# Attention norms with tokens on the partitions from block 4 on, in a fused attention and two-layer kernel

## The chip, the cores and the metric

The kernel runs on one core of one Trainium2 chip. The metric is the device time of one execution in microseconds; lower is better. Before the change three runs took 282.09, 282.47 and 282.67 us (median 282.47). The profiled execution took 282.48 us, and its span, from the first to the last instruction, is 280.7 us.

## What is computed

An attention without a softmax, a norm over each head, and a two-layer net with a leaky ReLU that has a slope of its own for each hidden unit:

```python
kv = np.einsum('bhsd,bhse->bhde', k, v)          # 8 batches, 8 heads, 576 tokens, 64 wide
out = np.einsum('bhsd,bhde->bhse', q, kv)
rms = np.sqrt(np.mean(out * out, axis=-1, keepdims=True) + 1e-06)
x = out / rms * g_norm                           # then to (4608 tokens, 512)
h = x @ w_in                                     # 512 -> 2048
g = np.maximum(h, 0.0) + alpha * np.minimum(h, 0.0)
return g @ w_out                                 # 2048 -> 512
```

Inputs and output are fp32; the matmuls run on fp16 copies with fp32 sums.

## The kernel before

**Blocks and units.** The 4608 tokens are worked on in nine blocks w of 512 (L39). A batch has 576 tokens, so a block spans a batch boundary in most cases. The main loop (L781) goes over the blocks, and inside a block over 16 units u (L784). A unit holds one first-layer group, `m1_group` (four 512-column matmuls on TensorE, L391; a ReLU of the negative on ScalarE, L398; the combination `gt` on VectorE, L402), seven 256-column matmuls of the second layer of the block before (`prod_mm`, L523; the product is done by a scheme with seven instead of eight sub-products, which needs sums of `gt` quarters, `s_sum`, L489, 16 a block on VectorE), and a piece of the attention for the block after (`attention(w + 1, u)`, L764). So the norms of block 4 are computed in the loop of block 3.

**Attention of a block, channels on partitions.** Heads go in pairs j = 0 to 3 (two heads of 64 fill 128 partitions). `step_kv` (L323) makes the 128x128 product kv of a pair from five matmuls, and VectorE copies it under a mask (L335). `step_ot` (L340) multiplies kv by the transposed queries: 512 columns for each pair, in two matmuls where the block spans two batches; the result has channels on partitions and tokens along the row. ScalarE squares it (L355). `ssq_mm` (L362) sums the squares over the 64 channels of a head with a 512-column matmul against a 0/1 mask (L365), and ScalarE takes the reciprocal root of all 128x512 values (L367). `norm` (L372) multiplies on VectorE by the gain `g2col` and by the root, and writes `xt`, the moving operand of the first layer, one tile for each pair. The units of these steps are written out by hand: kv at 1, 4, 7, 10, the product at 3, 6, 9, 12, sum and norm at 5, 8, 11, 14 (L753).

**Queries.** Batches 0 to 2 are transposed on TensorE (`step_t`, L287). From batch 3 on (`B_NAT`) `dma_t` (L312) sends five DMA transposes from SyncE's queue, each of 128 (the last of 64) tokens by 512 channels; the loop of block 1 issues those of batch 3 in unit 3 (L790), later loops those of batch w + 2 in unit 11 (L815).

**Order and buffers.** Each engine runs its instructions in the order of the program text, SyncE's and GpSimd's queues too. From block 2 on the first-layer results go to two PSUM banks in turn (L793), so a unit's first matmul waits until `gt` two units before has been computed. The attention products have two PSUM buffers ("o"). GpSimd issues the loads (L180); the load of the query remainder of batch w + 2 waits until the transposes of the batch before have read the shared buffer (L158). SyncE's queue also carries the output stores (L427).

Of the kernel before, what the change touches and what calls it, by code (L numbers as in the profile page):

```python
# [9 lines left out]
FP32 = mybir.dt.float32  # L10
FP16 = mybir.dt.float16
AF = mybir.ActivationFunctionType
ALU = mybir.AluOpType
# [4 lines left out]
def kernel(  # L18
# [11 lines left out]
    nc = tc.nc  # L30

    B, H, S, D = q.shape
# [3 lines left out]
    P = 128  # L36
    NPAIR = H // 2
    W = 512
    NW = N_TOK // W  # L39
    TPW = W // P  # L40
    TPP = S // P
    MAIN = TPP * P
    REM = S - MAIN
    NT = TPP + 1
# [3 lines left out]
    NC = D_MODEL // P  # L48
    assert NC == NPAIR and 0 < REM < P and P0 <= P and H % 4 == 0
    B_NAT = 3  # L50
    inv_d = 1.0 / D

    const_p = ctx.enter_context(tc.tile_pool(name="constp", bufs=1))
    w_p = ctx.enter_context(tc.tile_pool(name="weights", bufs=1))
    xt_p = ctx.enter_context(tc.tile_pool(name="xt", bufs=2))
# [63 lines left out]
    NBUF = 3  # L119
    HH = H // 2  # L120
    bufs = []
    for i in range(NBUF):
        t = {}
        for nm in ("k", "v", "q"):
            n = 1 if nm == "v" else T0 if i == 0 else NT
            t[nm] = qkv_p.tile([P, n, H, D], FP16, name=f"{nm}sb{i}")
            if i > 0 or nm == "v":
                nc.vector.memset(t[nm][REM:P, n - 1, :, :], 0.0)
        bufs.append(t)
# [26 lines left out]
            )  # L156

    def buf_of(b, nm):  # L158
        return bufs[1 if nm == "q" and b >= B_NAT else b % NBUF][nm]

    def load_rem(b, nm):
        nc.gpsimd.dma_start(  # L162
# [2 lines left out]
        )  # L165

    def regroup(b, nm, h0, h1, eng=None):
        dst = bufs[b % NBUF][nm][:, 0:TPP, h0:h1, :].rearrange("p t h d -> p h t d")
        src = stages[b, nm][:, h0:h1, :, :]
        if eng is nc.scalar:  # L170
            nc.scalar.copy(out=dst, in_=src)
        else:
            (eng or nc.vector).tensor_copy(out=dst, in_=src)

    def load_batch(b, names=("k", "v", "q")):
        for nm in names:
            load_rem(b, nm)
            load_main(b, nm)
# [30 lines left out]
    def load_w_in(i):  # L209
# [4 lines left out]
        )  # L214
        w_in_sb.append(t)

    def load_w_out(i):
        t = w_p.tile([P, GW, D_MODEL], FP16, name=f"w_out_sb{i}")
        nc.gpsimd.dma_start(
            out=t[:],  # L220
            in_=moe_w_out[i * GW * P : (i + 1) * GW * P, :].rearrange("(g p) m -> p g m", p=P),
        )
        w_out_sb.append(t)

    def w_in_blk(c, g):
        i = max(n for n, f0 in enumerate(IN_CUTS[:-1]) if f0 <= g * P)
        f0 = g * P - IN_CUTS[i]
        return w_in_sb[i][:, c, f0 : f0 + P]
# [20 lines left out]
    load_batch(1, ("v",))  # L249
    load_w_out(2)  # L250
    load_w_out(3)
    load_batch(2, ("q", "k", "v"))


    warm_ps = ps_q.tile([P, W], FP32, name="warm_ps", tag="q")
# [18 lines left out]
    def pair_cols(b, nm, j):  # L274
        def f(t):
            n = rows(b)
            if nm == "v" and b == 0:
                h = 2 * j % HH
                return stages[b, nm, 2 * j // HH][0:n, h : h + 2, t, :]
            if nm == "v" and t < TPP:  # L280
                return stages[b, nm][:, 2 * j : 2 * j + 2, t, :]
            if nm == "v":
                return bufs[b % NBUF][nm][0:n, 0, 2 * j : 2 * j + 2, :]
            return bufs[b % NBUF][nm][0:n, t, 2 * j : 2 * j + 2, :]
        return f

    def step_t(b, j, pool=(ps_s, "s")):  # L287
        qs = pair_cols(b, "q", j)
        qt_ps = pool[0].tile([P, n_runs(b) * rows(b)], FP16, name="qt_ps", tag=pool[1])
        c = 0  # L290
        for t in range(n_runs(b)):
            n = rows(b)
            nc.tensor.matmul(  # L293
                out=qt_ps[:, c : c + n],
                lhsT=qs(t),
                rhs=ident16[0:n, 0:n],
                is_transpose=True,
                start=(t == 0),
                stop=(t == n_runs(b) - 1),
            )  # L300
            c += n
        if j == 0:
            qt_all[b] = attn_p.tile([P, NPAIR, S], FP16, name="qt_all")
        qts[b, j] = qt_all[b][:, j, :]
        if b == 0 and j < 2:
            nc.vector.tensor_copy(out=qts[b, j], in_=qt_ps[:, 0:S])
        else:
            nc.scalar.copy(out=qts[b, j], in_=qt_ps[:, 0:S])

    qt_all = {}  # L310

    def dma_t(b):  # L312
        qt = attn_p.tile([P, NPAIR, S], FP16, name="qt_all")
        for t in range(NT):
            c0, c1 = t * P, min((t + 1) * P, S)
            src = stages[b, "q"][:, t] if t < TPP else buf_of(b, "q")[0:REM, TPP]
            nc.sync.dma_start_transpose(
                out=qt[:, :, c0:c1], in_=src.rearrange("p h d -> p (h d)"),
            )
        for j in range(NPAIR):  # L320
            qts[b, j] = qt[:, j, :]

    def step_kv(b, j, pool=(ps_s, "s")):  # L323
        ks, vs = pair_cols(b, "k", j), pair_cols(b, "v", j)
# [46 lines left out]

    def norm(w, j):  # L372
        ot_ps, rstd = ots.pop((w, j))
        xts[w, j] = xt_p.tile([P, W], FP16, name="xt", tag=f"xt{j}")
        nc.vector.scalar_tensor_tensor(  # L375
            out=xts[w, j][:], in0=ot_ps[:], scalar=g2col[:], in1=rstd[:],
            op0=ALU.mult, op1=ALU.mult,
        )

    gts = {}  # L380
# [8 lines left out]
    def m1_mm(h_ps, w, g, cs):  # L389
        for c in cs:  # L390
            nc.tensor.matmul(  # L391
                out=h_ps[:], lhsT=w_in_blk(c, g), rhs=xts[w, c][:],
                start=(c == 0), stop=(c == NC - 1),
            )

# [11 lines left out]
    def m1_group(w, g, pool=None):  # L407
        h_ps = pool[0].tile([P, W], FP32, name="h_ps", tag=pool[1]) if pool else h_bank()
        m1_mm(h_ps, w, g, range(NC))
        m1_evac(h_ps, w, g)  # L410
# [248 lines left out]
    ssq_mm(0, 3, h_at(2))  # L659
    norm(0, 2)  # L660
    norm(0, 3)
    first = [ps_h.tile([P, W], FP32, name="h_ps", tag=f"h{g}") for g in range(3)]
    for c in range(3):
        for g in range(2):
# [6 lines left out]
    for g in range(3, NF):  # L671
        m1_group(0, g, {3: S_POOL, 4: O_POOL, 5: O_POOL, 6: Q_POOL}.get(g))
        if g == 14:
            regroup(1, "k", 0, H)
            nc.vector.memset(bufs[0]["k"][REM:P, TPP, :, :], 0.0)


    ys = {}
# [65 lines left out]
        13: ((0, 1, 2), (0, 2, 2)),  # L744
    }

    def unit_sums(w, u):
        for back, n, k in S_AT.get(u, ()):
            if 1 <= w + back < NW:
                s_sum(w + back, n, k)  # L750

# [9 lines left out]
            ATT_1.setdefault(at, []).append((what, j))  # L761
    ATT = {"t": step_t, "kv": step_kv, "ot": step_ot, "ssq": step_ssq}

    def attention(w, u):  # L764
        if w < NW:
            for what, j in (ATT_1 if w == 2 else ATT_AT).get(u, ()):
                if what == "t" and w >= B_NAT:
                    continue
                if w < B or what in ("ot", "ssq"):
                    if w == 2 and what in ("kv", "ssq"):  # L770
                        pool = Q_POOL if j % 2 == 0 else S_POOL
                        (step_kv if what == "kv" else step_ssq)(w, j, pool)
                    else:
                        ATT[what](w, j)

    REG_AT = {8 + 2 * j: (("k", j),) for j in range(NPAIR)}

    Y3_AT = [(8, 8), (8, 8), (8, 8), (8, 9), (9, 9), (9, 10), (10, 10), (10, 10), (10, 11), (11, 11), (11, 12), (12, 12), (12, 13), (13, 14), (14, 16), (16, 16)]
    REG_2 = {2 * j: (("k", j),) for j in range(NPAIR)}
# [1 line left out]
    for w in range(1, NW):  # L781
        if w + 2 < B:
            load_gated(w + 2)
        for u in range(NF):  # L784
            m1_group(w, G_ORDER[u])
            if w > 1:
                unit_sums(w, u)
            if w == 1 and u == 2:
                regroup(2, "k", 0, H)
            if w == 1 and u == 3:  # L790
                dma_t(3)
            if w == 2 and u == 0:
                h_tags[0] = ("h1", "h2")  # L793
                h_turn[0] = 1
            if w > 2 and u == 0:
                y_read(w - 2, "c12")
            if w == 1:
                for i in range(*Y3_AT[u]):
                    y_mm(ys[3], 0, 3, i)
                    if i == NF - 1:  # L800
                        y_out(ys[3], 0, 3)
            else:
                for i in range(u * PER, (u + 1) * PER):
                    prod_mm(w - 1, *Y_LIST[i])
                for what in Y_READS.get(u, ()):
                    y_read(w - 1, what)
            attention(w + 1, u)
            if w == 1:
                for k in {5: (0,), 7: (1,)}.get(u, ()):
                    s_sum(1, 1, k)  # L810
                    s_sum(1, 2, k)
            if w + 2 < B:
                for nm, j in REG_AT.get(u, ()) if w > 1 else ():
                    regroup_pair(w + 2, nm, j)
                if u == 11 and w > 1:  # L815
                    dma_t(w + 2)
            if w == 2:
                for nm, j in REG_2.get(u, ()):
                    regroup_pair(3, nm, j)
                if u < 2:  # L820
                    s_sum(1, u + 1, 2)
# [48 lines left out]
```

## Time and profile before

| what | value |
|---|---|
| span of the profiled execution | 280.7 us |
| TensorE busy, granted clock | 274.0 us (98%), 1.0 throughout |
| VectorE, ScalarE, GpSimd busy | 219.9, 157.0, 61.9 us |
| loop of block 2 to 6, each | 28.89 us |
| loop of block 7, of block 8 | 27.77, 25.06 us |
| mask-sum matmuls L365 | 36 in all, 4 in a loop with attention |
| ScalarE roots L367, squares L355 | 690 and 598 ns each, 36 of each |
| VectorE norms L375 | 745 ns each, 36 |
| DMA transposes | 25, 2.3 us from issue to landing in the median |

In the profile a matmul's busy time overlaps with the next one's, so TensorE's cost is read from start to start. VectorE's instructions overlap a little too: the mean of one is longer than the distance between two that follow at once. A loop's length is the distance between the first first-layer matmuls of two blocks.

### The profile page before, as it was taken

The numbers are of one execution on the slowest core, as the hardware profiler recorded it, in microseconds if no ns is written. First come the engines' busy times: TensorE is split into PE (matmuls) and PEld (weight loads), VectorE is DVE, ScalarE is ACT, GpSimd is POOL, SyncE is SP. The second block draws the span as 40 slices with busy tenths as digits, with TensorE's granted clock in tenths as the row PEclk, the third lists the DMA queues.
The fourth block names the chain that finished last, engine by engine and source line by source line (L and its number), as shares of the span: only waits on it lengthen the run. The fifth ranks groups of instructions, "written<-read, shape, count | busy, mean of one in ns | idle before, by whom it ended". The sixth has DMA issues, their size and how long they took to land.

```text
span 280.7 us, 4978 instructions
## 1 busy us (share of the span) xinstructions
PE 274.0 (98%) x1888; PEld 173.8 (62%) x1888; DVE 219.9 (78%) x418; ACT 157.0 (56%) x268; POOL 61.9 (22%) x85
## 2 busy tenths in 40 slices
PE   7899999999999999999999999999999999999995
PEld 3444444555666676666666666666666666666784
DVE  6668729898788877887889787978887888787872
ACT  3567437788676545764576456745564566443310
POOL 8843332740720046007300450000000000000000
PEclk9999999999999999999999999999999999999999
DMA  8999999999793469947953697330112011201223
GB/s 163 199 207 196 197 201 193 191 140 169 91 171 69 104 72 165 152 112 120 165 91 97 121 152 122 93 106 1 40 37 75 2 37 37 77 0 37 77 76 114
DMA packets 77628, 31.37 MB, mean 112 GB/s; under 512 B 45780, under 2 KB 77284, under 8 KB 77604
## 3 DMA queue, kind: packets, MB, share of 16 engines
q0 software_dynamic: 55600, 18.85, 58.8%
q1 hardware_dynamic: 21108, 11.25, 15.0%
q10 hardware_dynamic: 896, 0.95, 1.0%
q8 instruction: 15, 0.25, 0.4%
q14 instruction: 9, 0.07, 0.1%
HBM read 36.71 MB, written 9.44 MB: 164 GB/s over the span
## 4 chain that ended last, share of the span: by engine, by line
PE 92%; DMA 5%; DVE 1%; ACT 0%; issue 0%; DVEq 0%
PE h_ps L391 42%; PE yY L546 15%; PE yZ L546 10%; PE yX L546 10%; DMA vst<-in_v_dram 5%; PE kv_ps L327 3%; PE ot_ps L349 3%; PE ssq_ps L365 3%; PE y L416 2%; PE warm_ps L259 2%; PE qt_ps L293 1%; DVE xt L375 1%; ACT rstd L367 0%; DVE kv_sb L335 0%; DVE ksb L193 0%
## 5 line engine op out<-in xcount | busy, mean ns | idle before, releaser
L391 PE MATMUL h_ps<-xt,w_in_sb 128*128 128x512 f16 x576 | 145.2, 379 | 0.2
L402 DVE SCALAR_TENSOR_TENSOR gt<-m_sb,beta_sb,h_ps 128x512 f16<-128x512 f32 x144 | 106.9, 746 | 39.9 <-ACT m_sb L398 38.1
L398 ACT ACTIVATE m_sb<-h_ps 128x512 f32<-128x512 f32 x144 | 86.0, 598 | 74.8 <-PE h_ps L391 60.2
L391 PEld LDWEIGHTS <-w_in_sb 128*128 128x128 f16 x576 | 54.8, 98 | 46.4 <-issue 1.0
L546 PEld LDWEIGHTS <-s 128*128 128x128 f16 x512 | 50.1, 98 | 19.3
L546 PEld LDWEIGHTS <-gt 128*128 128x128 f16 x384 | 37.6, 98 | 14.8
L546 PE MATMUL yY<-wsum,s 128*128 128x256 f16 x256 | 36.3, 273 | 0.0
L546 PE MATMUL yX<-w_out_sb,gt 128*128 128x256 f16 x256 | 35.1, 273 | 0.0
L355 ACT ACTIVATE sq_sb<-ot_ps 128x512 f16<-128x512 f32 x36 | 21.2, 598 | 16.7 <-PE ot_ps L349 16.6
L367 ACT ACTIVATE rstd<-ssq_ps,eps_t 128x512 f32<-128x512 f32 x36 | 24.7, 690 | 9.7 <-PE ssq_ps L365 9.2
L375 DVE SCALAR_TENSOR_TENSOR xt<-ot_ps,g2col,rstd 128x512 f16<-128x512 f32 x36 | 26.6, 745 | 3.2 <-ACT rstd L367 3.2
L162 POOL DMA_DIRECT2D qsb<-in_q_dram x7 | 4.9, 699 | 78.3 <-DMA qt_all<-qsb 76.3
L153 POOL DMA_DIRECT2D qst<-in_q_dram x20 | 17.7, 922 | 1.9 <-DMA vst<-in_v_dram 1.9
L546 PE MATMUL yZ<-wsum,s 128*128 128x256 f16 x128 | 17.6, 273 | 0.0
L546 PE MATMUL yZ<-w_out_sb,s 128*128 128x256 f16 x128 | 17.6, 273 | 0.0
L546 PE MATMUL yY<-wsum,gt 128*128 128x256 f16 x128 | 17.6, 273 | 0.0
L416 PE MATMUL y<-w_out_sb,gt 128*128 128x512 f16 x64 | 16.8, 379 | 0.5 <-DMA w_out_sb<-in_moe_w_out_dram 0.5
L349 PE MATMUL ot_ps<-qt_all,kv_sb 128*128 128x512 f16 (+7 forms) x64 | 13.6, 286 | 0.4 <-DVE kv_sb L335 0.3
L498 DVE TENSOR_TENSOR s<-s,gt 128x512 f16<-128x512 f16 x32 | 13.5, 421 | 0.5
L327 PEld LDWEIGHTS <-ksb 128*128 128x128 f16 (+1 forms) x164 | 11.5, 98 | 3.7 <-DVE ksb L193 1.1
L365 PE MATMUL ssq_ps<-sq_sb,mask 128*128 128x512 f16 x36 | 13.6, 379 | 0.1
L496 DVE TENSOR_TENSOR s<-gt 128x512 f16<-128x512 f16 x32 | 13.3, 419 | 0.1
(66 smaller groups left out, 206.6 us busy)
## 6 DMA issues: line engine op xcount, KB each, us to landing
out_dram<-y_sb SPq DMA_DIRECT2D x19, 256.0 KB, 2.2
kst<-in_k_dram POOLq DMA_DIRECT2D x7, 512.0 KB, 7.8
vst<-in_v_dram POOLq DMA_DIRECT2D x7, 512.0 KB, 9.9
qst<-in_q_dram POOLq DMA_DIRECT2D x20, 128.0 KB, 7.2
w_out_sb<-in_moe_w_out_dram POOLq DMA_DIRECT2D x4, 512.0 KB, 16.1
out_dram<-y_sb SPq DMA_DIRECT2D x25, 64.0 KB, 4.2
w_in_sb<-in_moe_w_in_dram POOLq DMA_DIRECT2D x3, 512.0 KB, 11.6
out_dram<-y_sb SPq DMA_DIRECT2D x9, 128.0 KB, 2.1
```

Of the source, the lines that this page charges most:

```text
L153: nc.gpsimd.dma_start(out=st[:, t, :, :], in_=srcs["q"][b, :, t * P : (t + 1) * P, :].rearrange("h p d -> p h d"),)
L327: nc.tensor.matmul(out=kv_ps[:], lhsT=ks(t), rhs=vs(t), start=(t == 0), stop=(t == n_runs(b) - 1),)
L349: nc.tensor.matmul(out=ot_ps[:, n0 - w * W : n1 - w * W], lhsT=kvs[b, j][:], rhs=qts[b, j][:, n0 - b * S : n1 - b * S], start=True, stop=True,
L355: nc.scalar.activation(out=sq[:], in_=ot_ps[:], func=AF.Square)
L365: nc.tensor.matmul(out=ssq_ps[:], lhsT=mask16[:], rhs=sq[:], start=True, stop=True)
L367: nc.scalar.activation(out=rstd[:], in_=ssq_ps[:], func=AF.Abs_reciprocal_sqrt, bias=eps_t[:], scale=inv_d,)
L375: nc.vector.scalar_tensor_tensor(out=xts[w, j][:], in0=ot_ps[:], scalar=g2col[:], in1=rstd[:], op0=ALU.mult, op1=ALU.mult,)
L391: nc.tensor.matmul(out=h_ps[:], lhsT=w_in_blk(c, g), rhs=xts[w, c][:], start=(c == 0), stop=(c == NC - 1),)
L398: nc.scalar.activation(out=m_sb[:], in_=h_ps[:], func=AF.Relu, scale=-1.0)
L402: nc.vector.scalar_tensor_tensor(out=gts[w, i][:, r, :], in0=m_sb[:], scalar=beta_sb[:, g : g + 1], in1=h_ps[:], op0=ALU.mult, op1=ALU.add,)
L416: nc.tensor.matmul(out=y[:], lhsT=gt_cols(w, g, a * P, (a + 1) * P), rhs=w_out_blk(g), start=(g == 0), stop=(g == NF - 1),)
L546: nc.tensor.matmul(out=bank, lhsT=lhs, rhs=rhs, start=fresh, stop=(c == NK - 1), skip_group_check=True,)
```

## The change

From block 4 on (`W_ROW = 4`) the attention product, its norm and the transposition of the result are done another way; block 4 to 8 are 20 tiles of 128 tokens.

- `rows_mm`: for each tile of 128 tokens four 128-column matmuls (one for each pair), with the transposed queries as the stationary and kv as the moving operand, fill one "o" bank with tokens on partitions and all 512 channels along the row. A tile that spans two batches takes two matmuls for each pair, the halves of the query tile being padded with zeros; there are two such tiles. ScalarE squares the bank.
- `rows_ssq`: VectorE sums the squares of each head (`tensor_reduce`, 128x512 to 128x8), two units later.
- `rows_rs`, `rows_norm`: three units after the product ScalarE takes the root of 128x8 values, VectorE multiplies the bank by the roots spread over each head, and SyncE's queue sends a DMA transpose of the 128x512 result into `xt`, now one tile of all four pairs. The mask matmul and the wide root are gone for these blocks.
- The gain moves into `w_in`: in the loop of block 2, VectorE scales the 128x4x128 weights of each group in place, right after that group's evacuation, so `norm` of block 3 leaves the gain out.
- In the loops of blocks 3 to 7 kv moves to units 0, 0, 1, 2 (the second one in an "o" buffer), products to 3, 5, 7, 9, sums of squares to 5, 7, 9, 11, roots and norms to 6, 8, 10, 12; six of the `gt` sums move to later units and two to earlier ones (from unit 6 to 4). The query transposes of batch w + 2 are spread over units 8, 9, 10 and 12, after the result transposes of the same unit; those of batches 3 and 4 go to unit 12.
- The transposed queries lie in two fixed buffers with zeroed padding; batch 2 uses batch 0's query buffer, so its loads stand later in the program; k regroups on ScalarE move from units 8, 10, 12, 14 to 9, 11, 13, 15.

```diff
@@ -213,6 +214,14 @@
+    def scale_w_in(g):
+        ...
+        blk = w_in_sb[i][:, :, f0 : f0 + P]
+        nc.vector.tensor_scalar(
+            out=blk, in0=blk, scalar1=g2col[:], scalar2=None, op0=ALU.mult,
+        )
@@ -249,7 +258,6 @@
-    load_batch(2, ("q", "k", "v"))
@@ -371,10 +378,72 @@
     def norm(w, j):
         ot_ps, rstd = ots.pop((w, j))
-        xts[w, j] = xt_p.tile([P, W], FP16, name="xt", tag=f"xt{j}")
+        if w >= W_ROW - 1:
+            nc.vector.tensor_mul(out=xt_cols(w, j), in0=ot_ps[:], in1=rstd[:])
+            return
         nc.vector.scalar_tensor_tensor(
-            out=xts[w, j][:], in0=ot_ps[:], scalar=g2col[:], in1=rstd[:],
+            out=xt_cols(w, j), in0=ot_ps[:], scalar=g2col[:], in1=rstd[:],
             op0=ALU.mult, op1=ALU.mult,
+        )
+
+    def rows_mm(w, i):
+        n0 = w * W + i * P
+        b, r = divmod(n0, S)
+        o_ps = ps_o.tile([P, W], FP32, name="or_ps", tag="o")
+        for j in range(NPAIR):
+            cols = o_ps[:, j * P : (j + 1) * P]
+            if r + P <= S:
+                c = PAD + r
+                nc.tensor.matmul(
+                    out=cols, lhsT=qt_sb[b % 2][:, j, c : c + P], rhs=kvs[b, j][:],
+                    start=True, stop=True,
+                )
+            else:
+                ...
+        sq = attn_p.tile([P, W], FP16, name="sq_sb")
+        nc.scalar.activation(out=sq[:], in_=o_ps[:], func=AF.Square)
+        ...
+    def rows_ssq(w, i):
+        ...
+        nc.vector.tensor_reduce(
+            out=ssq[:], in_=sq[:].rearrange("p (h d) -> p h d", h=H),
+            axis=mybir.AxisListType.X, op=ALU.add,
+        )
+        ...
+    def rows_rs(w, i):
+        ...
+        nc.scalar.activation(
+            out=rstd[:], in_=ssq[:], func=AF.Abs_reciprocal_sqrt, bias=eps_t[:], scale=inv_d,
+        )
+        ...
+    def rows_norm(w, i):
+        ...
+        nc.vector.tensor_tensor(
+            out=xr[:], in0=o_ps[:].rearrange("p (h d) -> p h d", h=H),
+            in1=rstd[:].unsqueeze(2).to_broadcast([P, H, D]), op=ALU.mult,
+        )
+        xt_cols(w, 0)
+        nc.sync.dma_start_transpose(
+            out=xts[w][:, :, i * P : (i + 1) * P], in_=xr[:].rearrange("p h d -> p (h d)"),
         )
@@ -672,7 +742,11 @@
         if g == 14:
             regroup(1, "k", 0, H)
-            nc.vector.memset(bufs[0]["k"][REM:P, TPP, :, :], 0.0)
+            for nm in ("k", "q"):
+                nc.vector.memset(bufs[0][nm][REM:P, TPP, :, :], 0.0)
+            for t in qt_sb:
+                nc.vector.memset(t[:, :, 0:PAD], 0.0)
+                nc.vector.memset(t[:, :, PAD + S : PAD + S + PAD], 0.0)
@@ -744,8 +818,16 @@
+    S_ROW = dict(S_AT)
+    for at, what in (
+        (4, ((-1, 3, 3), (0, 1, 0), (0, 2, 0))), (6, ()), (7, ((-1, 4, 0),)), (8, ((-1, 4, 1),)),
+        (9, ()), (10, ((-1, 4, 2),)), (11, ()), (12, ((-1, 4, 3),)),
+        (13, ((0, 1, 1), (0, 2, 1))), (15, ((0, 1, 2), (0, 2, 2))),
+    ):
+        S_ROW[at] = what
@@ -761,8 +843,27 @@
+    for what, ats in (
+        ("kv", (0, 0, 1, 2)), ("mm", (3, 5, 7, 9)), ("ssq", (5, 7, 9, 11)),
+        ("rs", (6, 8, 10, 12)), ("norm", (6, 8, 10, 12)),
+    ):
+        for j, at in enumerate(ats):
+            ATT_ROW.setdefault(at, []).append((what, j))
+    QT_AT = {8: (0,), 9: (1,), 10: (2,), 12: (3, 4)}
...
@@ -783,12 +884,12 @@
             m1_group(w, G_ORDER[u])
+            if w == W_ROW - 2:
+                scale_w_in(G_ORDER[u])
...
-            if w == 1 and u == 3:
-                dma_t(3)
@@ -805,6 +906,8 @@
             attention(w + 1, u)
+            if w == 1 and u == 12:
+                dma_t(3)
@@ -812,7 +915,7 @@
-                if u == 11 and w > 1:
+                if u == 12 and 1 < w < W_ROW - 1:
                     dma_t(w + 2)
```

## The prediction

> **What bounds the kernel now.** I read the page's busy line and chain first, then the windows of single loops, then the timeline of one loop.
>
> ```profile
> PE 274.0 (98%) x1888; PEld 173.8 (62%) x1888; DVE 219.9 (78%) x418; ACT 157.0 (56%) x268; POOL 61.9 (22%) x85
> ...
> PE 92%; DMA 5%; DVE 1%; ACT 0%; issue 0%; DVEq 0%
> ```
>
> The chain of waits that ended last is 92% TensorE (PE). The windows (busy time of each engine, one row for each loop of blocks 2 to 7) show the same without a gap:
>
> ```profile
> 66.83:95.72 28.89, 28.89 (x209) 19.42 (x208) 24.06 (x47) 19.65 (x35) 7.32 (x9) 1.00 0.90 115
> 95.72:124.61 28.89, 28.89 (x210) 19.50 (x208) 23.65 (x46) 17.38 (x31) 7.33 (x9) 1.00 0.99 126
> 124.61:153.51 28.90, 28.90 (x211) 19.46 (x208) 23.66 (x46) 17.39 (x31) 7.32 (x9) 1.00 0.88 115
> ...
> 211.29:239.06 27.77, 27.77 (x186) 18.00 (x184) 22.89 (x42) 15.65 (x27) 0.00 (x0) 1.00 0.11 38
> ```
>
> TensorE is busy for the whole of each loop at full clock, so a loop is as long as its matmuls. VectorE (third engine) is busy 23.7 of 28.9 us: 5.2 us are free, so it is the next bound. What each matmul costs is read from starts in the timeline of TensorE:
>
> ```profile
> 137.00 0.38 PE L349 MATMUL ot_ps<-qt_all,kv_sb 128*128 128x320 f16 x2
> 137.22 1.03 PE L391 MATMUL h_ps<-xt,w_in_sb 128*128 128x512 f16 x4
> 138.08 0.93 PE L546 MATMUL yY<-wsum,s 128*128 128x256 f16 x7
> 138.85 0.39 PE L327 MATMUL kv_ps<-vst,ksb 128*128 128x128 f16 x4
> 139.07 0.22 PE L327 MATMUL kv_ps<-vsb,ksb 128*128 128x128 f16 x1
> 139.12 1.03 PE L391 MATMUL h_ps<-xt,w_in_sb 128*128 128x512 f16 x4
> ```
>
> Start to start: 512 columns 0.216 us (0.86/4), 256 columns 0.109 (0.77/7), five 128-column matmuls 0.27, so 0.056 each; the product of one pair 0.22. A bare unit is 4 x 0.216 + 7 x 0.109 = 1.63 us. VectorE's timeline:
>
> ```profile
> 140.82 0.75 DVE L402 SCALAR_TENSOR_TENSOR gt<-m_sb,beta_sb,h_ps 128x512 f16<-128x512 f32 x1 [0.62 <-ACT m_sb L398]
> 141.48 0.42 DVE L502 TENSOR_TENSOR s<-gt,s 128x512 f16<-128x512 f16 x1
> ...
> 143.56 0.42 DVE L502 TENSOR_TENSOR s<-gt,s 128x512 f16<-128x512 f16 x1
> 143.90 0.68 DVE L568 TENSOR_TENSOR u<-yY,p 128x512 f32<-128x512 f32 x1
> 144.51 0.75 DVE L402 SCALAR_TENSOR_TENSOR gt<-m_sb,beta_sb,h_ps 128x512 f16<-128x512 f32 x1
> ```
>
> Start to start: `gt` 0.66, a sum 0.34, an output addition (L568) 0.61. Unit by unit, `gt` can start 1.05 us after the unit's last first-layer matmul (140.82 against 139.12 + 3 x 0.216).
>
> **What the skill says.** "VectorE: DVE Perf Modes", section The perf-mode tier table: `tensor_reduce` has the 1x mode only, `tensor_scalar` on fp16 in SBUF the 4x mode; its section on the TRN2 errata prices an SBUF instruction at (58 + elements/mode)/0.96 ns. The trace agrees where it can: a 512-element sum at 2x gives 0.340 us (measured 0.34), the 2048-element copy L173 at 4x 0.594 (measured 0.60 start to start). No row shows a reduce. "TensorE: Matmul & The Clock Gate", Back-to-back issue gap, has N/2.4 + 2.5 ns for an isolated matmul, 56 ns at 128 columns, but about 81 ns in a stream with weight loads. The kv matmuls here, each with its own weights, take 56, and the measurement decides. "DMA: Bandwidth & Descriptors", Anatomy of one DMA, gives about 2.0 us fixed for a DMA; the 25 transposes here land after 2.3 us in the median, 5.0 at most.
>
> **The change part by part**, for the five loops of blocks 3 to 7; u+0 is the start of unit u's last first-layer matmul.
>
> *TensorE.* Removed: 20 mask matmuls x 0.216 = 4.32 us, and 20 pair products x 0.219 = 4.38. Added: 18 tiles x 4 and 2 boundary tiles x 8 = 88 matmuls x 0.056 = 4.93. Sum: **-3.77 us**, all on the path. kv is moved, not changed.
>
> *ScalarE* loses the wide roots (690 ns each) and gets 128x8 ones, at most as long. It has 11 us free in a loop: nothing.
>
> *VectorE* gets a reduce for each tile. Unknown; not under 0.34 (the 2x sum), not over the 0.75 of a three-operand instruction on PSUM; I take (58 + 512)/0.96 = 0.60. The norm becomes a two-operand instruction like L568: 0.61 apart, 0.685 long (upper end L375's 0.745). A loop's VectorE time becomes 23.7 + 4 x 0.60 - 4 x 0.06 = 25.8 of about 28.2: no bound in sum, but it counts where TensorE waits. Its queue, unit by unit:
> - Unit 4: `gt`, three sums (one on another's result, +0.08): 1.05 + 0.66 + 1.02 + 0.08 = 2.81; the next `gt` is ready at 1.63 + 1.05 = 2.68: 0.13 late. Unit 5: `gt`, addition, reduce = 1.87 against 1.63 + 0.22 (four row matmuls) = 1.85: 0.15 late. Unit 6: norm 0 ends at 1.05 + 0.15 + 0.66 + 0.69 = 2.55.
> - The row products of unit 7 need norm 0's PSUM buffer. TensorE comes there at 0.22 + 0.76 + 0.86 + 0.76 = 2.61; with 0.05 for the signal norm 0 gives 2.60. No wait.
> - Unit 8: `gt`, a sum, norm 1: 1.05 + 0.66 + 0.34 + 0.69 + 0.05 = 2.79. The products of unit 9 come at 2.61: **wait 0.18**, with unit 10's group, weight loads apart, queued behind it. Five loops: **+0.9 us**. Ends: 0 (norm sooner by that much), and 0.24 in unit 9 with 0.20 in unit 7 where norm and reduce are at their upper ends, 2.2 us.
> - `gt` may be late by the distance to the matmul that reuses its bank, 0.6 us in the tightest unit before; here 0.13 to 0.25.
> - kv of pair 2 in unit 1 needs the PSUM buffer of pair 0: VectorE, after `gt`, a sum and an addition, has masked it at 1.05 + 0.66 + 0.34 + 0.61 + 0.29 = 2.95 from unit 0; TensorE comes at 1.63 + 2 x 0.28 + 0.98 = 3.17. No wait.
>
> *The result transposes.* Each occupies SyncE's queue 1.2 us. Nine in a loop are 11 us; the stores behind them have no reader, and GpSimd's next loads still wait for the last query transpose, now two issues behind result transpose 3, about where it was. The first query transpose of a loop stands behind result transpose 1, four microseconds into unit 8, at about 143.8 in block 4's loop; the queries it reads had landed there by 140.8. Norm 2 needs the buffer that result transpose 0 has read, four units before. Only the last result transpose is near the path: units 11 (`gt`, addition, reduce: 1.87 against 1.63, 0.24 late) and 12 (`gt`, sum, norm 3) end norm 3 at 1.05 + 0.24 + 0.66 + 0.34 + 0.69 = 2.98; SyncE takes 0.02, landing 2.3, the signal 0.05: 5.35. The next block's first matmul comes at 0.98 + 3 x 1.63 = 5.87. **0.5 us to spare**, so nothing; upper end 5.0 us for landing, priced below.
>
> *Scaling `w_in`.* 16 instructions in block 2's loop; the skill's 4x price is (58 + 128)/0.96 = 0.19 us, the lower end; the upper is 1x, 0.60. At 0.19, 3.1 us go into 4.8 free ones; carrying 0.19 behind each `gt` through that loop's VectorE timeline leaves the last norm 0.24 late, at 96.19, before the fourth matmul of block 3 at 96.37 reads it. Nothing.
>
> *Edits of no cost.* The zeroing of five paddings (the present one takes 0.27 us; at most 1.4) delays the q regroup at 32.4 by up to 1 us; TensorE then waits for a weight DMA until 35.0 and for v until 38.1, which hides it. Batch 2's loads: GpSimd reaches them at 29.6 us and their new wait, batch 0's transposes, ended by 12. The transposes of batches 3 and 4: that SyncE instruction already waits for block 2's products in unit 12 (it starts at 63.2), so the later place changes nothing. The later k regroups have ScalarE's free time and a free unit before kv.
>
> Sum: 280.7 - 3.77 + 0.9 = 277.8 of span; the profiled run was 282.48 beside a median of 282.47: **279.6 us**, 1.0% faster.
>
> **The rivals.**
> - *No wait at all*: norm 1 is sooner by 0.18. 278.7. The margin is a tenth of a unit; against it stands the trace's regular timing.
> - *Longer VectorE work, or whole-tile waits*: reduce and norm at the upper ends give 280.9. If a block's first matmul also waits for all of `xt`, because it is one tile now, blocks 0, 2 and 3 lose about 0.3 to 0.8 us each: up to 282. I take 281.
> - *Slower: the last result transpose comes late.* At the start of blocks 4 to 8 TensorE then stands still. It costs from a landing of 2.8 us on, and at (0.5 + 2.9/5) more than 2.3, 3.4 us, the gain is gone. Halfway between the median and the slowest, 3.65, each block loses 0.85: 283.9. For it: the transposes at 63.2 took 5.0 under full DMA load. Against: those at 177.5, right behind a 256 KB store, took 2.35, and in units 12 to 15 the loads are still held back.
> - *The change does not get the fast mode for scaling* (0.60 each): 16 x 0.41 = 6.6 us more overrun the loop; TensorE loses about 3.5 by the last norm of block 3: 283.1.
>
> **How the numbers follow.** Forecast 0.52, no wait 0.15, longer work 0.14, late transpose 0.09, slow scaling 0.04, and 0.06 that mixtures end within 0.2%, about what a measurement here can tell from no change (281.9 to 283.0). Faster 0.81, same 0.06, slower 0.13. The range 278.5 to 281.9 takes in the first three with 0.81.
>
> **What would show it.** The loops of blocks 3 to 7 become 28.3 us (27.2 for block 7) from 28.9 and 27.8, those of blocks 1, 2 and 8 stay; the row matmuls 0.056 apart; a wait of some 0.2 us in unit 9 on VectorE's norm and none in unit 7; reduces of 0.6 to 0.7 us; result transposes landing in 2.3 us; no gap at a block's start. It is wrong if TensorE stops for a DMA at block starts, or VectorE's idle time is gone.

## The result, and the profile after

The changed kernel takes 284.39 us (median of 4 runs, 284.25 to 285.03) beside 282.57 of the kernel before (4 runs, 282.09 to 283.06): **0.7% slower**, ratio 1.0069, 95% interval 1.0046 to 1.0092. The forecast was 279.6, in a range from 278.5 to 281.9. The profiled execution has a span of 283.1 us, 2.4 more than before. One run among the experiments below (290.99 us, at a granted clock of 0.987) belongs to a slower state of the chip and is left out of their figures.

The page's busy line and the chain of the changed kernel:

```profile
PE 272.0 (96%) x1920; PEld 173.4 (61%) x1920; DVE 234.0 (83%) x458; ACT 148.9 (53%) x268; POOL 62.3 (22%) x85
...
PE 66%; DMA 20%; DVE 7%; issue 2%; POOL 2%; ACT 1%; SPq 0%; DVEq 0%; POOLq 0%
```

TensorE's share of the chain fell from 92% to 66%, and DMA's rose from 5% to 20%. That is not 15% of time lost: TensorE worked beside most of these transfers. It says that the chain, followed back from the end, now passes through loads (those of v make 14% of it) where it passed through matmuls. Where, the windows of single loops tell (start and end; length; then busy time of each engine, TensorE first). The loops of blocks 2 to 5:

```profile
66.65:97.66 31.01, 29.23 (x209) 19.37 (x208) 28.18 (x62) 19.48 (x35) 7.32 (x9) 1.00 0.92 110
97.66:127.79 30.13, 28.70 (x214) 19.16 (x212) 25.92 (x50) 16.23 (x32) 7.33 (x9) 1.00 1.17 142
127.79:156.95 29.16, 28.59 (x216) 19.39 (x217) 25.90 (x50) 15.83 (x30) 7.32 (x9) 1.00 1.03 135
156.95:185.17 28.22, 28.21 (x213) 19.22 (x213) 24.96 (x49) 15.26 (x30) 7.33 (x9) 1.00 1.08 142
```

Before, these were 28.89 each, with TensorE busy throughout. Two things stand out. The loop of block 2, which has no row products at all, became 2.1 us longer. And the gain that was forecast is there only where nothing stops TensorE (28.22 in block 5's loop); the loops of blocks 3 and 4 lose it again in gaps. Taken from start to start in the timeline of TensorE, the stops that the forecast did not have are:

| where | us | what TensorE waited for |
|---|---|---|
| loop of block 2, at 71.80 | 1.89 | the load of v of batch 3 |
| same loop, at 79.3 | 0.22 | VectorE |
| loop of block 3, at 122 to 124 | 1.31 | `gt`, itself late behind a norm |
| first matmul of blocks 4, 5, 8 | 0.60, 0.72, 0.49 | the last result transpose |

They add up to 5.23 us. With the five waits in unit 9 and the saving on TensorE as forecast, +0.9 - 3.77 + 5.23 = +2.4 us: the whole difference of the two profiled spans (the medians differ by 1.8). The first row, in TensorE's timeline:

```profile
69.14 0.93 PE L615 MATMUL yX<-w_out_sb,gt 128*128 128x256 f16 x7
71.80 0.38 PE L334 MATMUL kv_ps<-vst,ksb 128*128 128x128 f16 x4 [1.73 <-DMA vst<-in_v_dram]
```

The transfer that it waits for is not one that the change moved. SyncE's queue shows what happened beside it, the transposes of the queries of batch 3. Before:

```profile
63.24 5.23 SPq L317 DMA_TRANSPOSE qt_all<-qst  x4
68.57 1.20 SPq L317 DMA_TRANSPOSE qt_all<-qsb  x1
```

After:

```profile
56.30 7.91 SPq L324 DMA_TRANSPOSE qt_sb<-qst  x4
64.30 1.20 SPq L324 DMA_TRANSPOSE qt_sb<-qsb  x1
```

They start 7 us *earlier*, although their place in the program is later. The load of v is issued at 58.7 and at 58.5. Its landing, before and after:

```profile
DMA to landing us min/median/max: 8.9/8.9/8.9
...
DMA to landing us min/median/max: 13.2/13.2/13.2
```

The result transposes, by their line (who waited for them, and issue to landing):

```profile
  DVE x_rows L440: 1.6, 1
  PE h_ps L460: 1.3, 3
...
DMA to landing us min/median/max: 2.4/2.4/8.3
```

The median is as forecast; the maximum is not.

### The profile page after: what moved, and what is told of

It reads as the page before. It is cut to its first block, busy times and chain, and to the rows that moved or that the text cites. A ratio compares the mean times of both kernels' runs of the same rounds, so it can differ in the third digit from the quotient of the medians.

```text
span 283.1 us, 5149 instructions
## 1 busy us (share of the span) xinstructions
PE 272.0 (96%) x1920; PEld 173.4 (61%) x1920; DVE 234.0 (83%) x458; ACT 148.9 (53%) x268; POOL 62.3 (22%) x85
## 4 chain that ended last, share of the span: by engine, by line
PE 66%; DMA 20%; DVE 7%; issue 2%; POOL 2%; ACT 1%; SPq 0%; DVEq 0%; POOLq 0%
PE h_ps L460 30%; DMA vst<-in_v_dram 14%; PE yY L615 12%; PE yX L615 9%; PE yZ L615 7%; DMA xt<-x_rows 3%; PE kv_ps L334 3%; DMA out_dram<-y_sb 2%; PE warm_ps L267 2%; DVE gt L471 2%; PE or_ps L402 2%; POOL qst L154 1%; DVE x_rows L440 1%; PE ssq_ps L372 1%; DVE w_in_sb L222 1%
## 5 line engine op out<-in xcount | busy, mean ns | idle before, releaser
L417 ACT ACTIVATE sq_sb<-or_ps 128x512 f16<-128x512 f32 x20 | 12.0, 601 | 6.7 <-PE or_ps L402 5.9
L440 DVE TENSOR_TENSOR x_rows<-or_ps,rstd_r 128x512 f16<-128x512 f32 x20 | 13.7, 683 | 1.6 <-DMA xt<-x_rows 1.6
L334 PE MATMUL kv_ps<-vst,ksb 128*128 128x128 f16 (+1 forms) x136 | 12.2, 219 | 2.1 <-DMA vst<-in_v_dram 2.1
L362 ACT ACTIVATE sq_sb<-ot_ps 128x512 f16<-128x512 f32 x16 | 9.3, 598 | 8.8 <-PE ot_ps L356 8.6
L342 DVE TENSOR_TENSOR kv_sb<-kv_ps,mask 128x128 f16<-128x128 f32 x32 | 8.7, 284 | 6.3 <-PE kv_ps L334 6.3
L423 DVE TENSOR_REDUCE ssq_r<-sq_sb 128x8 f32<-128x512 f16 x20 | 13.5, 676 | 0.0
```

What stands on the lines that cost most here:

```text
L334: nc.tensor.matmul(out=kv_ps[:], lhsT=ks(t), rhs=vs(t), start=(t == 0), stop=(t == n_runs(b) - 1),)
L362: nc.scalar.activation(out=sq[:], in_=ot_ps[:], func=AF.Square)
L417: nc.scalar.activation(out=sq[:], in_=o_ps[:], func=AF.Square)
L423: nc.vector.tensor_reduce(out=ssq[:], in_=sq[:].rearrange("p (h d) -> p h d", h=H), axis=mybir.AxisListType.X, op=ALU.add,)
L440: nc.vector.tensor_tensor(out=xr[:], in0=o_ps[:].rearrange("p (h d) -> p h d", h=H), in1=rstd[:].unsqueeze(2).to_broadcast([P, H, D]), op= ...
```

## The experiments

Three causes were put to the test; the letters in the expectations stand for each experiment's own pair. **Early transposes**: the fixed query buffers let batch 3's transposes start early, and these slow the load of v. **Loads**: result transposes in the loop of block 3 share the DMA engines with the loads of batch 5, and land late. **The queue**: SyncE's queue, in which a query transpose and a store stand ahead, holds back the last result transpose of a loop. What each kernel took, beside the kernel before on the same chip:

| kernel | us, median (range, runs) | before | ratio, 95% interval |
|---|---|---|---|
| batch 3's transposes reordered | 283.89 (282.83 to 284.74, 12) | 282.85 | 1.0032, 1.0016 to 1.0047 |
| before, with fixed query buffers | 285.55 (284.27 to 286.05, 5) | 282.85 | 1.0081, 1.0054 to 1.0109 |
| three row buffers | 285.70 (283.97 to 287.77, 8) | 282.85 | 1.0086, 1.0054 to 1.0118 |
| norms ahead of the sums | 287.44 (284.91 to 287.50, 3) | 282.85 | 1.0127, 1.0076 to 1.0178 |
| batch 4's reordered as well | 282.87 (282.24 to 283.68, 12) | 282.66 | 1.0008, 0.9996 to 1.0020 |
| row 5, third query transpose late | 280.96 (280.27 to 282.03, 6) | 282.66 | 0.9942, 0.9922 to 0.9963 |
| row 5, norms first | 282.06 (281.30 to 284.21, 20) | 282.66 | 0.9984, 0.9971 to 0.9997 |
| all of these together | 280.33 (279.29 to 280.70, 6) | 282.66 | 0.9918, 0.9902 to 0.9935 |
| all, shorter warm-up | 280.30 (279.79 to 281.51, 6) | 282.66 | 0.9927, 0.9907 to 0.9947 |
| no scaling of `w_in` | 285.94 (1 run) | 282.66 | not compared |

A profile is one execution. That of the kernel after was the slowest of its four runs (285.03), that of the first reordering near the fastest of its twelve (283.07). So stops are counted in the profiles below, and what an edit is worth as a whole is read from the medians.

### The start of batch 3's transposes

In the kernel after, the transpose of the fourth query tile goes first. It overwrites columns that block 2's last product still reads, so it waits for unit 12, and with the edit the others wait behind it in SyncE's queue:

```diff
-                dma_t(3)
+                dma_t(3, (3, 4, 0, 1, 2))
```

> The changed kernel with one edit: the five query transposes of batch 3 in the order 3, 4, 0, 1, 2. Tile 3 must wait for block 2's products, so the first three, which now start at 56.3 us, can start only behind it, near 63 us. Theory A (the fixed query buffers let three transposes run early, among the loads of k and v of batch 3, and v comes 4 us later, at 71.8): v lands near 67.6, the wait of 1.7 us of TensorE at 71.8 is gone, the loop of block 2 takes 28.9 to 29.2 us instead of 31.0, the time is about 282.3. Theory B (the scaling of w_in on VectorE, or the moved loads of batch 2, lengthen this loop): the loop stays at 31.0 and the time at 284.4.

SyncE's queue and the landing of v:

```profile
63.14 1.30 SPq L324 DMA_TRANSPOSE qt_sb<-qst  x1
64.49 1.24 SPq L324 DMA_TRANSPOSE qt_sb<-qsb  x1
65.77 3.89 SPq L324 DMA_TRANSPOSE qt_sb<-qst  x3
...
DMA to landing us min/median/max: 9.8/9.8/9.8
```

v landed 9.8 us after its issue (13.2 before the edit), and the stop at 71.8 was gone: the loop of block 2 took 29.11, of which 0.21 us was still a wait, for a VectorE sum at 72. The loop of block 3 still took 30.23, and blocks 4, 5 and 8 still started late by 0.4 to 0.6. The time fell short of theory A, though: 283.89, not 282.3. With each taken beside the kernel before on its own chip, the edit gained 0.8 us, less than the stop of 1.89 in the one profile of the kernel after; in two other kernels with the early transposes (three row buffers, norms ahead of the sums) the stop was 1.47 and 1.56.

The same cause put alone into the kernel *before*: its query buffers are made fixed, and all query transposes go to unit 12, as in the change. Norms, products and scaling stay as they were:

```diff
+    qt_sb = [const_p.tile([P, NPAIR, S], FP16, name=f"qt_sb{i}") for i in range(2)]
...
-        qt = attn_p.tile([P, NPAIR, S], FP16, name="qt_all")
+        qt = qt_sb[b % 2]
...
-            if w == 1 and u == 3:
-                dma_t(3)
+            if w == 1 and u == 12:
+                dma_t(3)
...
-                if u == 11 and w > 1:
+                if u == 12 and w > 1:
```

> The kernel before with one part of the change alone: two fixed buffers for the transposed queries instead of tiles from a pool, and all query transposes issued in unit 12; no padding, no row products, no scaling. Theory A: the transposes of batch 3 start near 56 us instead of 63, v of batch 3 lands near 71.5 instead of 67.6, the loop of block 2 grows from 28.9 to about 30.8 us and the time to 284.4. Theory B: nothing moves, 282.5.

Its transposes started at 56.9, and v of batch 3, issued at 59.0, landed after 14.0 us. What waited for v, and its landing:

```profile
  PE kv_ps L325: 2.8, 1
...
DMA to landing us min/median/max: 14.0/14.0/14.0
```

The loop of block 2 grew to 31.81, by 2.92; every other loop stayed at 28.89 or 27.77. The early transposes are shown as a cause from both sides: without them the stop is gone, and this part alone makes the kernel before slower by 2.7 us, more than the whole change did (1.8).

### The loop of block 3

VectorE's timeline of the kernel after, in the loop of block 3:

```profile
120.69 0.69 DVE L440 TENSOR_TENSOR x_rows<-or_ps,rstd_r 128x512 f16<-128x512 f32 x1 [1.65 <-DMA xt<-x_rows]
```

Norm 2 stands 1.65 us because its row buffer is still being read by result transpose 0, issued at 112.26 and landed 8.3 us later; there are two such buffers. Everything behind it on VectorE is late, `gt` too, and TensorE stops. A third buffer takes that wait away:

```diff
-        xr = attn_p.tile([P, H, D], FP16, name="x_rows")
+        xr = attn_p.tile([P, H, D], FP16, name="x_rows", bufs=3)
```

> The changed kernel with three row buffers instead of two. Theory A (in the loop of block 3 norm 2 waits 1.65 us for the buffer that result transpose 0 still reads, since that transpose lands only after 8.3 us behind the loads of batch 5; VectorE stands, its next evacuations are late, TensorE loses 1.3 us): VectorE's wait is gone, the loop of block 3 shrinks from 30.1 to about 28.9 us, and block 4's start still waits 0.3 to 0.7 us for result transpose 3; time 283.0 to 283.4. Theory B (the late transposes cost the same wherever they are waited for): what the loop of block 3 gains, the start of block 4 loses, time 284.2 or more.

The stop in the loop of block 3 was gone, but the first matmul of block 4 waited 1.62 us instead of 0.60, the loop still took 29.84, and the kernel was no faster (285.70). So the buffer was not the cause, only the place where the late transposes were felt first.

Next, in the kernel with batch 3's order, batch 4's transposes are sent in an order that lets its remainder go first, which frees the shared remainder buffer for batch 5's loads sooner:

```diff
-                    dma_t(w + 2)
+                    dma_t(w + 2, (4, 3, 0, 1, 2))
```

> As the run with batch 3's transposes reordered, and batch 4's transposes in the order 4, 3, 0, 1, 2, so that the one that frees the query buffer for GpSimd goes first. Theory A (result transposes of block 4 land after 8 us because the loads of batch 5, begun at 103, still run until 122): the loads begin near 98.5 and end near 118, result transposes 0 and 1 of block 4 land within 3 to 5 us, VectorE's wait of 1.6 us and the wait at the start of block 4 are gone, the loop of block 3 shrinks from 30.2 to 28.3 us, the time to about 282.0. Theory B (the transposes are slow whatever is beside them there): the loop stays at 30.

The load of v of batch 5 was issued at 103.3 instead of 108.5 and landed at 115.1 instead of about 122. Result transposes 0, 1 and 2 landed in 7.0, 4.4 and 2.4 us (8.5, 8.3 and 4.2 without this edit), and TensorE's stop in the middle of this loop was gone (1.41 us without the edit). That the late landings and this stop go with the loads is shown. But the loop took 29.67, not 28.3: block 4 now started 1.45 us late instead of 0.58. The total came down to that of the kernel before.

How much this loop varies, a kernel shows that was made for another question. It has batch 3's order alone, and leaves out the scaling of `w_in`, so that the gain is missing from block 3 on:

```diff
-            if w == W_ROW - 2:
-                scale_w_in(G_ORDER[u])
```

> The changed kernel with the query transposes of batch 3 in the order 3, 4, 0, 1, 2, and without the scaling of w_in: the gain is left out of the norm from block 3 on. Theory A (the 16 scalings are hidden, as predicted): the loop of block 2 stays at 29.1 us. Theory B (the 0.2 us that TensorE waits at 72.0 for a sum of VectorE comes from the scaling ahead of it): 28.9.

The loop of block 2 took 28.89, as before the change: the remaining 0.21 us there was the scaling. In the loop of block 3 result transpose 0 was issued 14.6 us after the loop's start, as in the kernel with the scaling, and landed after 10.2 us instead of 8.5; TensorE stopped for 2.96, and the loop took 32.86. So a landing under these loads is no constant, even at the same place. Some of the loss is a lower clock: TensorE's was 0.95 in this loop, with 512-column matmuls 0.43 us apart for some 3 us after the stop. It is one execution, and only its loop of block 2 is used below.

### The last result transpose

SyncE's queue in the loop of block 4, kernel after:

```profile
151.45 2.21 SPq L324 DMA_TRANSPOSE qt_sb<-qst  x1
153.76 0.54 SPq L496 DMA_DIRECT2D out_dram<-y_sb  x1
154.40 1.23 SPq L445 DMA_TRANSPOSE xt<-x_rows  x1
```

And the norm that the third line sends on, in VectorE's timeline:

```profile
152.74 0.68 DVE L440 TENSOR_TENSOR x_rows<-or_ps,rstd_r 128x512 f16<-128x512 f32 x1
```

The norm ended at 153.42, the queue was held until 154.3, first by the third query transpose and then by a store, and the result landed 2.42 us after its issue, at 156.81. Block 5's first matmul ran at 156.95.

The place in the queue does not explain this alone. In the loop of block 5 the same transpose and store stood ahead of the last result transpose, and the norm ended the same 1.97 us after that query transpose was issued. There the query transpose held the queue for 1.21 us instead of 2.21, and the result transpose left 0.03 us after its norm. In the loop of block 4 an instruction fetch (a transfer of 16 KB) began at 152.06, 0.6 us after the query transpose was issued. All seven profiles with a third query transpose in unit 10 agree: 1.90 to 2.23 us in the loop of block 4, each time with a fetch 0.57 to 0.65 us after the issue, and 1.21 in the loop of block 5, without one. No run here moves the fetch and keeps this order, so its part is read from the traces, not tested.

The test sends that query transpose behind the result transpose, in the kernel with both orders:

```diff
-    QT_AT = {8: (0,), 9: (1,), 10: (2,), 12: (3, 4)}
+    QT_AT = {8: (0,), 9: (1,), 12: (2, 3, 4)}
```

> The kernel with the reordered query transposes of batches 3 and 4 (282.87, span 281.6), and in the loops of blocks 3 to 7 the third query transpose issued in unit 12, behind the last result transpose, instead of in unit 10. Theory A: SyncE's queue, held by that query transpose and a store, delays the last result transpose; then blocks 4 and 5 start without the waits of 1.45 and 0.68, the five waits of 0.18 in unit 9 stay, and the time is about 280.9. Theory B: the landing under other traffic makes these waits, whatever stands ahead in the queue; then they stay and the time is within 0.4 of 282.9.

Its queue in the same loop:

```profile
148.22 0.54 SPq L496 DMA_DIRECT2D out_dram<-y_sb  x1
150.21 1.21 SPq L445 DMA_TRANSPOSE xt<-x_rows  x1
151.52 2.52 SPq L324 DMA_TRANSPOSE qt_sb<-qst  x2
```

The result transpose left as soon as its norm was there. Block 5 started without a wait and block 4 with 0.16; only block 8's 0.36 stayed, and the five waits of 0.18 in unit 9. The kernel took 280.96, 1.9 us less than without the edit, as theory A had it. What stands ahead in the queue is shown as a cause. Block 4 needs no fetch for it: without this edit its last result transpose left 1.14 us after the norm, behind a query transpose of 1.21 and two stores. Block 5 had the lengthened query transpose as well. Of the separate edits this one gained the most.

The other way to gain time for the last transpose is a norm that comes sooner. In the loops of blocks 3 to 7 the `gt` sums of units 8, 10 and 12 are put behind the norm:

```diff
-            if w > 1:
+            late = W_ROW - 1 <= w < NW - 1 and u in (8, 10, 12)
+            if w > 1 and not late:
                 unit_sums(w, u)
...
             attention(w + 1, u)
+            if late:
+                unit_sums(w, u)
```

First in the kernel after, with nothing else:

> The changed kernel with one edit: in units 8, 10 and 12 of the loops of blocks 3 to 7 VectorE's sum comes behind the norm instead of before it. Theory A (the 0.18 us that the row products of unit 9 wait are the time by which the sum ahead of norm 1 makes it late): norm 1 ends 0.34 us sooner, the five waits of 0.18 us are gone, norm 3 ends 0.34 us sooner too, which shortens the wait at the start of block 8 by about 0.3; time about 283.2. Theory B (VectorE is full, and what norm 1 gains the next evacuation loses): the waits turn up at the first-layer matmuls instead, 284.4.

The five waits in unit 9 were gone (the loops of blocks 5 and 6 took 28.05 and 28.27). The stops at v, in the loop of block 3 and at block 5 stayed, block 4's fell to 0.27, and block 8's grew to 1.03, where the last result transpose landed after 4.06 us. The expected 283.2 was missed by far; but the granted clock was 0.992 and 0.993 in the two longer runs, so the time is not read as an effect of the edit. Then in the kernel with both orders:

> The same kernel with the norms ahead of the sums in units 8, 10 and 12, the third query transpose left in unit 10. Theory A (as above): the five waits of 0.18 in unit 9 go, which is 0.9, and the norms end some 0.35 sooner, but the queue still delays the last result transpose in blocks 4 and 5 by 0.3 to 1.1; the time is about 281.5. Theory B: the norm that is 0.35 sooner takes away most of the waits at the starts as well, and the time is 280.3, that of the kernel with all of it together.

282.06, above both expectations and nearer the first. The trace has no wait in unit 9, but 0.43 at block 4 and 0.58 at block 5, where the queue is still held, and 1.47 at block 8, to which the next section comes. The sooner norm is worth 0.8 us here, the freed queue 1.9.

### All together, and block 8

Both orders, the late query transpose and the norms first:

> The edits together: the order of batch 3's and batch 4's query transposes, in later loops query transpose 2 behind result transpose 3 (unit 12 instead of 10), and VectorE's sum behind the norm in units 8, 10 and 12. Theory A (five places, each with its own wait): beside what the two orders give, the waits of 0.18 us in unit 9 are gone (0.9 us) and the wait of 0.4 to 0.7 us at block 5's start is gone; only block 8's start still waits, 0.5 to 1.0; loops of blocks 4 to 7 28.1 to 28.2 and 27.1 to 27.5; time 280.5, faster than the kernel before. Theory B (the gain is given back elsewhere, in evacuations or later loads): not under 282.

280.33, **0.8% faster than the kernel before** (0.9902 to 0.9935); no other kernel was faster beyond the noise. The windows of the loops of blocks 3, 4 and 7:

```profile
96.70:124.75 28.05, 28.05 (x215) 19.23 (x213) 25.57 (x49) 15.90 (x32) 7.42 (x9) 1.00 1.15 151
124.75:153.02 28.27, 28.27 (x218) 19.46 (x216) 25.62 (x49) 15.92 (x32) 7.32 (x9) 1.00 1.06 143
...
209.34:236.90 27.56, 27.10 (x195) 18.06 (x193) 25.27 (x46) 14.02 (x27) 0.00 (x0) 1.00 0.22 59
```

In the first two TensorE has no gap again; the third ends with 0.62 us of waiting at the start of block 8. There the last result transpose was issued in time, but landed after 3.65 us, with no load near. In the DMA view of the kernel after (queue; packets, MB, share of 16 engines), from the issue of its own, which landed after 3.18, the only other transfer is again an instruction fetch:

```profile
q1 hardware_dynamic: 511, 0.13, 33.2%
q8 instruction: 1, 0.02, 3.0%
```

To move the fetches without touching the loops, the matmuls at the start of the program whose results nothing reads (`keep_warm`) become six wide and 26 narrow ones instead of ten wide ones:

```diff
-    keep_warm(10)
+    keep_warm(6)
+    for i in range(26):
+        nc.tensor.matmul(
+            out=warm_ps[:, 0:64], lhsT=warm16[:, 0:P], rhs=warm16[:, 0:64], start=True, stop=True,
+        )
```

> As the run with all edits, with 22 more weight load and matmul pairs at the program's start[...] (four wide ones become 26 narrow ones). They move the 16 KB fetches of TensorE's instructions, one every 17 us, by 44 of 256 instructions, about 3 us earlier. Theory A (result transpose 3 of block 8 lands 0.8 to 1.6 us late because such a fetch falls on it at 238): the fetch falls near 235, that transpose lands in 2.4 us and the start of block 8 waits for nothing; 0.5 to 1.0 us faster than without the shift, unless another last transpose is hit. Theory B (something else makes it late): no change.

The fetch came at 231.1 instead of 233.7. It now met result transpose 2 (3.3 us); result transpose 3 landed in 2.40, and block 8 started without a wait. But another fetch, at 179.5, came 1.9 us behind the last result transpose of the loop of block 5, and block 6 started 1.27 us late. TensorE also stopped for 0.72 us in the loop of block 3, as it did not in the profile with all the edits. The time did not change: at block 8 the wait was gone, and elsewhere there was another.

## Why the prediction was wrong, step by step

**The step that failed first** was the query transposes, which the prediction put at no cost: "that SyncE instruction already waits for block 2's products in unit 12 (it starts at 63.2), so the later place changes nothing". The wait was read from the trace as a property of the instruction. It belonged to the buffer: a tile from a pool of two, handed over as a whole once its last reader is done. The fixed buffers, an edit that the prediction had listed for their padding alone, are waited for by region, and only the columns of the last two tiles were still in use. So three transposes left 7 us sooner, the load of v came 4 us later, and 1.9 us of TensorE went (in this profile). The reordering and the kernel before with this part alone show it.

**Result transposes beside loads.** "Norm 2 needs the buffer that result transpose 0 has read, four units before" took a landing of 2.3 us. In the loop of block 3, transposes 0 and 1 took 8.3 and 7.8, because they are issued in units 6 to 8, where batch 5's loads run; the prediction had looked at units 12 to 15 alone. That cost 1.3 us on TensorE. The Trainium skill says in "DMA: Bandwidth & Descriptors", section Issuing engines are not separate DMA queues, that transfers started by different engines run on the same 16 DMA engines and interleave. The traces fit this: v's load, issued within 0.2 us of the same moment, landed in 8.9, 13.2 or 9.8 us by where the transposes stood.

**"SyncE takes 0.02"** for the last result transpose. In the loop of block 4 it was held for 1.0 us, in that of block 3 for 0.3 behind a norm that was late itself. Nine transposes of 1.2 us were counted for the queue as a whole and found harmless; that one of them stands just ahead of the last result transpose was not put into its sum, nor that it may take 2.2 us instead of 1.2. It ate the 0.5 us to spare. The skill's "Advanced Engine Details and Errata", section X-Bar Transpose (TRN2), calls transpose DMAs "as fast as regular DMAs": for an undisturbed landing the trace agrees (2.40 us beside 2.2 of a store of 256 KB), for the time in the issuing queue it does not (1.19 beside 0.53), and here the time in the queue decided.

**The rival of the late last transpose** named the right place, but priced it as a longer landing in each block. Undisturbed, the landing was 2.40 us; blocks 4 and 5 lost to the queue (0.60 and 0.72), block 8 beside a fetch (0.49), and blocks 6 and 7 lost nothing. That TensorE would stop for a DMA at block starts was the prediction's own sign of being wrong, and it came true.

**Scaling `w_in`**, set at 0.19 us each and nothing in sum, costs 0.2 us: the loop of block 2 is 29.11 with it and 28.89 without. The price was too low: in the kernel with batch 3's order one starts 0.26 us before the instruction that follows at once (and is 0.35 long), and in the kernel after four of the sixteen start 0.38 to 0.77 before it; why is open.

**What was right.** The saving on TensorE: the loops of blocks 3 to 7 in the kernel with all the edits together take 28.05 + 28.27 + 28.05 + 28.27 + 27.56, less 0.62 of waiting at block 8, against 4 x 28.89 + 27.77 before: 3.75 us less (3.77 forecast). The five waits of unit 9 are 0.175 to 0.178 each (0.18). The reduce is 0.676 us long and 0.60 from start to start, the norm 0.683, the row matmuls 0.056 apart, and unit 7 has no wait. Apart from the scaling, every price of an engine's instruction held; what failed were three statements about when a transfer starts and what it meets.

## What to carry to other kernels

When a buffer changes its kind, ask of every transfer that writes it which wait it loses and when it will start then: a start that moves sooner can cost more than one that moves later, since the load it meets is paid for by someone else. For a short transfer on the path, add up what stands ahead of it in its queue at that moment, not in a loop's total, and look at the loads at the time of each of them, not of the last alone. A wait that only moves when a buffer is added (0.60 to 1.62 at block 4) is the sign that its cause lies upstream.

## What the runs showed that was not expected

An instruction fetch (one transfer of 16 KB, mostly 14 to 20 us after the one before) goes with a late landing of a DMA transpose that is in flight. In ten profiles, the kernel after and nine of its variants, 60 result transposes were issued after 190 us, when no loads run, and have a recorded landing. With no fetch beginning within 2.4 us of the issue, 41 landed in 2.40 or 2.41 us. With a fetch that began within 2.1 us after the issue, all 15 landed in 2.97 to 4.57 us; with one from 2.2 us on, all 4 in 2.40 or 2.41. (In eight of the 15 a second fetch, of 8 KB, lay within 0.2 us of the issue; the other seven had the 16 KB alone.) Where the fetch came 1.9 to 2.0 us after the issue they took 4.4 to 4.6; the late start of block 6 in the last experiment fits this (1.9 us, and TensorE went on 4.4 us after the issue), but that transpose's own landing is not recorded. The last experiment moved the fetches, and the delay moved with them; which part of the hardware the two share stays open. The longer time in the queue before block 5 (2.2 us instead of 1.2) fits the same picture.
